# Dense layer of a fused attention, expert and dense kernel: activation buffers of 8 blocks, another order of the products, and a square that reads PSUM

## The chip, the cores and the metric

The kernel runs on one core of a Trainium2 chip. The metric is the device time of one execution in microseconds (us). Engines: PE is TensorE (matmuls), ACT is ScalarE, DVE is VectorE, POOL is GpSimd, SP issues most of the DMAs. [...]

## What is computed

Attention with queries pooled by two, then a layer of 8 experts with one expert for each token, then a dense layer. The change touches the dense layer alone:

```python
def _moe2_ref(x, w_in, w_out):      # x 2304 x 512, w_in 512 x 2048, w_out 2048 x 512
    h = x @ w_in
    r = np.maximum(h, 0.0)
    g = r * r
    return (g @ w_out).astype(np.float32)

def reference(**kwargs):
    ...
    attn_out = _attn_ref(**attn_kwargs)
    x = np.ascontiguousarray(attn_out.transpose(0, 2, 1, 3)).reshape(B * S, H * D)
    x = _moe_ref(x=x, **moe_kwargs)
    return _moe2_ref(x=x, **moe2_kwargs)
```

## The kernel before

Each f32 operand is held as two 16-bit halves, high and low, and each product is three matmuls (high x high, high x low, low x high). The dense layer is class Ffn. Its tokens are cut into 6 token blocks of 384 (N), the 2048 hidden columns into 16 blocks f of 128.

A first product of token block tt and column block f, here called a group, is the method hidden: 12 matmuls of 384 columns into one PSUM bank (L1465), then a relu on ACT into r in SBUF (L1470), the square on DVE in place (L1471), and one group later the high half on ACT (L1482) and the low half on POOL (L1483), which go to gh and gl. r has 3 buffers. The banks come from two pools, ps_b with 3 and ps_a with 2, chosen by f modulo 5. The function first(tt) runs the groups of a token block; of block 0 the first 8 (F1) have been done already, between the steps of the expert stage, into the tile fill (method step, the same hidden).

The function second(tt) makes three tiles of 128 tokens, each of 48 matmuls of 512 columns into a bank of ps_o (L1543); DVE scales the result (L1550) and POOL scatters it to the output with an indirect DMA (L1553).

The weights w_out arrive as 64-bit numbers in 16 blocks of 128 rows and are converted while first(0) and first(1) run: for each block three DVE instructions that put an f32 together (L1154, L1159, L1163), a copy of the high half on ACT (L1168) and a subtraction for the low half on POOL (L1170). The generator convert has six steps for each block (one is empty), and every group of the token blocks 0 and 1 takes four of them. The DMA of a later block (L1147) is issued by SP when a block is converted.

The instructions of each engine run in the order in which the program issues them; there is no planner in this part, the loops at the end of the method run are the order. All of them first do first(0), then first(tt + 1) ahead of second(tt). gh and gl of a token block are one tile each, of all 16 blocks, with two buffers.

Of the kernel before, what the change touches and what calls it, by code (L numbers as in the profile page):

```python
# [8 lines left out]
F32 = mybir.dt.float32  # L9
F16 = mybir.dt.float16  # L10
# [4 lines left out]
ALU = mybir.AluOpType  # L15
# [579 lines left out]
NTOK = 2304  # L595
# [3 lines left out]
F1 = 8  # L599
# [40 lines left out]
def half(w, lo):  # L640

    return w.bitcast(BF16) if lo else w
# [162 lines left out]
class Moe:  # L805
# [592 lines left out]
    def hidden(self, f2, ps, w1, x, w):  # L1398

        for f in range(2):  # L1400
            m = 0
            for k in range(4):
                fs = slice(256 * k + 128 * f, 256 * k + 128 * f + 128)
                for wh, xh in ((0, 0), (0, 1), (1, 0)):
                    self.nc.tensor.matmul(  # L1405
                        out=ps[:, f, 0:w], lhsT=w1(wh, f2)[:, fs], rhs=x[:, 4 * xh + k, 0:w],
                        start=(f == 0 and m == 0), stop=(m == 11), skip_group_check=True,
                    )
                    m += 1
# [15 lines left out]
class Ffn:  # L1425
# [3 lines left out]
    N = 384  # L1429
# [28 lines left out]
    def hidden(self, tt, f, ps, r, gh, gl):  # L1458
        nc = self.nc
        c0 = slice(tt * self.N, tt * self.N + self.N)  # L1460
        fs = slice(128 * f, 128 * f + 128)
        m = 0
        for k in range(4):
            for wh, yh in ((0, 0), (0, 1), (1, 0)):
                nc.tensor.matmul(  # L1465
                    out=ps, lhsT=half(self.win[wh][:, k, fs], wh), rhs=self.yT[yh][:, k, c0],
                    start=(m == 0), stop=(m == 11),
                )
                m += 1
        nc.scalar.activation(out=r, in_=ps, func=ACTF.Relu)  # L1470
        nc.vector.tensor_tensor(out=r, in0=r, in1=r, op=ALU.mult)  # L1471
        self.pend.append((r, gh, gl))
        if len(self.pend) > 1:
            self.halves()
# [10 lines left out]
    def run(self, ctx):  # L1485
        nc, moe, N = self.nc, self.moe, self.N
        pool = lambda n, b, **kw: ctx.enter_context(moe.tc.tile_pool(name=n, bufs=b, **kw))
        stg = pool("stg2", 2)
        one = pool("one", 1)
        gp = pool("gp", 2)  # L1490
        rp = pool("rp", 3)
        ps_o = pool("ps_o", 3, space=PSUM, reuse_waits="tile")
        ps_b = pool("ps_b", 3, space=PSUM, reuse_waits="tile")
        ps_a = pool("ps_a", 2, space=PSUM, reuse_waits="tile")
        wout = [one.tile([128, 16, 512], F16, name=f"wo{i}") for i in range(2)]
        cm = one.tile([128, 18, 2], F32, name="cms")
        nc.sync.dma_start(out=cm, in_=moe.cm.rearrange("(t p) m -> p t m", p=128))  # L1497
        ti = one.tile([128, 18], I32, name="ti")
        nc.vector.tensor_copy(out=ti, in_=cm[:, :, 1])
        so = {}  # L1500

        def wout_load(n):
            so[n] = stg.tile([128, 1024], U32, tag="g64", name="g64")
            moe.load64(so[n], moe.w_out[128 * n:128 * n + 128, :], nc.sync)

        def convert():
            for n in range(16):
                f = stg.tile([128, 512], U32, tag="f32", name="f32")
                split = moe.split64(so.pop(n), f, wout[0][:, n], wout[1][:, n])
                for i, _ in enumerate(split):  # L1510
                    yield
                    if i == 2:
                        yield
                if n + 2 < 16:
                    wout_load(n + 2)
                yield

        wout_load(0)
        wout_load(1)
        conv = convert()  # L1520
        G = {}

        def first(tt):
            gh, gl = G[tt] = [gp.tile([128, 16, N], F16, tag=t, name=t) for t in ("gh", "gl")]
            for f in range(0 if tt else F1, 16):
                ps = (ps_a if f % 5 in (3, 4) else ps_b).tile([128, N], F32, tag="a", name="a")
                r = rp.tile([128, N], F32, tag="r", name="r")
                self.hidden(tt, f, ps, r, gh[:, f], gl[:, f])
                if tt < 2:
                    for _ in range(4):  # L1530
                        next(conv, None)
            self.finish()

        def second(tt):
            g = G.pop(tt)
            at = lambda l, f: g[l][:, f] if tt or f >= F1 else self.g0[:, l, f]
            for rt in range(3):
                ps = ps_o.tile([128, 512], F32, tag="o", name="o")
                rs = slice(128 * rt, 128 * rt + 128)
                m = 0  # L1540
                for f in range(16):
                    for l, wh in ((0, 0), (0, 1), (1, 0)):
                        nc.tensor.matmul(  # L1543
                            out=ps, lhsT=at(l, f)[:, rs], rhs=half(wout[wh][:, f], wh),
                            start=(m == 0), stop=(m == 47),
                        )
                        m += 1
                n = 3 * tt + rt
                o = rp.tile([128, 512], F32, tag="o", name="ot")
                nc.vector.tensor_scalar(  # L1550
                    out=o, in0=ps, scalar1=cm[:, n, 0:1], scalar2=None, op0=ALU.mult
                )
                nc.gpsimd.indirect_dma_start(  # L1553
                    out=moe.out, out_offset=bass.IndirectOffsetOnAxis(ap=ti[:, n:n + 1], axis=0),
                    in_=o, in_offset=None, bounds_check=NTOK - 1,
                )

        first(0)
        for tt in range(NTOK // N):
            if tt + 1 < NTOK // N:  # L1560
                first(tt + 1)
            second(tt)


class First:
# [317 lines left out]
```

## Time and profile before

| | |
|---|---|
| median of 3 runs | 1180.41 us (1174.77 to 1183.54) |
| profiled execution, its own time | 1168.99 us |
| its span, first to last instruction | 1167.0 us |
| mean granted PE clock | 0.948 of full speed |
| busy share of the span: PE, DVE, ACT, POOL | 90%, 63%, 45%, 45% |

The span is what the trace covers; the execution's time has 2.0 us around it. Shares of busy time are means over stages with different limits, attention first, then the experts, then from about 771 us the dense layer. The views below give times in us from the start of the span. An instruction is named by engine and line, out<-in by the program's tiles; what stands in brackets behind it is the idle time of its engine before it and what ended that. [...]

### The profile page before, as it was taken

What the parts mean: (1) busy time and instruction counts of PE and PEld (TensorE: products, weight loads), DVE (VectorE), ACT (ScalarE), POOL (GpSimd) and SP (SyncE); (2) the same over time, 40 slices, a digit from 0 to 9 for tenths busy, and PEclk for the clock granted to TensorE, in tenths of its full rate; (3) what the DMA queues carried; (4) which work ended last, traced back from release to release, by engine and by line L of the source; (5) the groups of instructions that cost most, each with busy time, mean ns of one, the idle gap of its engine ahead of it and who ended that gap; (6) DMA issues with size and microseconds to landing.
All of it is one profiled execution on the core that took longest, in us unless ns stands there. A gap on an engine that the chain in (4) does not pass through costs nothing. (4 is left out here: it accounts for less than half of the span.)

```text
span 1167.0 us, 28582 instructions
## 1 busy us (share of the span) xinstructions
PE 1046.6 (90%) x11297; PEld 702.0 (60%) x11340; DVE 734.8 (63%) x1403; ACT 521.7 (45%) x972; POOL 519.3 (45%) x454
## 2 busy tenths in 40 slices
PE   6889999988999798999998869787879999999996
PEld 2455665655666466999898858654435454555543
DVE  6898999999999988866654547958822121211200
ACT  4777777767777566323222325533303131221300
POOL 3655564555666456522442336826623232232300
PEclk7899998999999898999999889989889999999999
DMA  7555875755675435659558595323300000000000
GB/s 195 141 130 145 201 169 108 170 147 118 140 151 150 72 96 161 166 176 224 103 111 210 135 256 167 89 72 111 111 19 10 19 10 10 19 10 19 1 28 27
DMA packets 166245, 128.17 MB, mean 110 GB/s; under 512 B 125208, under 2 KB 129432, under 8 KB 166064
## 3 DMA queue, kind: packets, MB, share of 16 engines
q1 hardware_dynamic: 160304, 107.91, 39.0%
q0 software_dynamic: 5760, 17.85, 5.0%
q8 instruction: 113, 1.85, 0.7%
q14 instruction: 68, 0.56, 0.2%
HBM read 74.69 MB, written 12.60 MB: 75 GB/s over the span
## 5 line engine op out<-in xcount | busy, mean ns | idle before, releaser
L422 POOL TENSOR_TENSOR pl<-p 128x512 f16<-128x512 f32 x144 | 167.9, 1170 | 176.2 <-ACT p L412 173.3
L394 PE MATMUL st<-r,t 128*128 128x64 f16 (+3 forms) x1152 | 202.6, 299 | 5.4 <-ACT p L412 4.7
L412 ACT ACTIVATE p<-st 128x512 f32<-128x512 f32 x288 | 168.5, 595 | 78.9 <-PE st L394 77.1
L1465 PE MATMUL a<-yT,win 128*128 128x384 f16 x1056 | 178.5, 332 | 16.8 <-ACT r L1470 11.8
L459 PEld LDWEIGHTS <-p 128*128 128x128 bf16 x2304 | 135.6, 99 | 68.1 <-issue 18.5
L1465 PEld LDWEIGHTS <-win 128*128 128x128 f16 (+1 forms) x1152 | 114.8, 100 | 97.3 <-issue 27.1
L459 PE MATMUL pv<-vx,p 128*128 128x65 f16 x2250 | 160.0, 197 | 9.5 <-DVE xb L500 9.5
L1543 PE MATMUL o<-wo,gh 128*128 128x512 f16 (+1 forms) x513 | 154.5, 380 | 5.7 <-ACT wo L1168 4.2
L459 PE MATMUL pv<-vx,pl 128*128 128x65 f16 x1125 | 144.9, 194 | 0.0
L422 DVE TENSOR_TENSOR pl<-p 128x512 f16<-128x512 f32 x144 | 141.8, 985 | 1.0 <-ACT p L412 0.7
L1470 ACT ACTIVATE r<-a 128x384 f32<-128x384 f32 x88 | 42.9, 487 | 194.8 <-PE a L1465 128.7
L1483 POOL TENSOR_TENSOR gl<-r,gh 128x384 f16<-128x384 f32 x88 | 87.3, 997 | 79.8 <-ACT gh L1482 79.8
L1471 DVE TENSOR_TENSOR r<-r 128x384 f32<-128x384 f32 x88 | 59.5, 676 | 100.2 <-ACT r L1470 100.2
L364 DVE CUSTOM_DVE_ANT_0 rd<-sm,rd,mc 128x512 bf16<-128x512 f32 x144 | 106.7, 744 | 22.4 <-PE sm L338 9.1
L1405 PE MATMUL fsm<-x,ws 128*128 128x192 f16 (+1 forms) x1344 | 104.7, 241 | 17.6 <-issue 9.8
L1550 DVE TENSOR_SCALAR ot<-o,cms 128x512 f32<-128x512 f32 x18 | 13.5, 751 | 166.5 <-PE o L1543 166.5
L394 PEld LDWEIGHTS <-t 128*128 128x128 f16 (+1 forms) x1152 | 77.0, 100 | 66.5 <-issue 32.0
L1405 PEld LDWEIGHTS <-ws 128*128 128x128 f16 (+1 forms) x1344 | 100.6, 101 | 20.8 <-issue 12.2
L459 PEld LDWEIGHTS <-pl 128*128 128x128 f16 x1152 | 111.0, 101 | 0.0
L361 ACT ACTIVATE rd<-sm 128x512 bf16<-128x512 f32 x144 | 85.5, 597 | 52.7 <-PE sm L338 43.6
L1417 PEld LDWEIGHTS <-ws 128*128 128x128 f16 (+1 forms) x1344 | 97.5, 99 | 18.1 <-issue 14.5
L1417 PE MATMUL fst<-hl,ws 128*128 128x192 f16 (+1 forms) x448 | 96.9, 236 | 12.7 <-issue 8.8
(249 smaller groups left out, 1735.3 us busy)
## 6 DMA issues: line engine op xcount, KB each, us to landing
stg<-in_moe_w SPq DMA_DIRECT2D x24, 1024.0 KB, 7.7
vr<-in_v SPq DMA_DIRECT2D x16, 576.0 KB, 4.2
kr<-in_k SPq DMA_DIRECT2D x15, 576.0 KB, 5.3
fill<-in_moe_w_in POOLq DMA_DIRECT2D x16, 512.0 KB, 7.0
g<-in_moe_w_out SPq DMA_DIRECT2D x16, 512.0 KB, 3.5
qr<-in_q SPq DMA_DIRECT2D x15, 512.0 KB, 5.7
t<-t SPq DMA_DIRECT2D x16, 288.0 KB, 3.8
xs<-tmp SPq DMA_DIRECT2D x16, 192.0 KB, 2.8
```

What stands on the lines that cost most here:

```text
L361: nc.scalar.activation(out=s["rd"], in_=ps, func=ACTF.Relu)
L364: nc.vector.tensor_tensor_reduce(out=rd, in0=ps, in1=rd, scale=1.0, scalar=mc[:, slots:slots + 1], op0=ALU.add, op1=ALU.max, accum_out=mx[ ...
L394: nc.tensor.matmul(out=st[:, j * n:j * n + n], lhsT=lhs[0:kk, m, :], rhs=r[0:kk, c0:c0 + n], start=first, stop=(kk == 65), skip_group_chec ...
L412: nc.scalar.activation(out=p, in_=st[:, 0:p.shape[1]], func=ACTF.Exp, scale=SCALE)
L422: eng.tensor_tensor(out=pl, in0=s.pop(("p32", i)), in1=s["ph", i], op=ALU.subtract)
L459: nc.tensor.matmul(out=o[:, 0:vn], lhsT=s[p, i][:, cs:cs + w], rhs=vx[:, 9 * a_ + c, v0:v0 + vn], start=(u == 0 and p == "ph" and v0 == 0) ...
L1405: self.nc.tensor.matmul(out=ps[:, f, 0:w], lhsT=w1(wh, f2)[:, fs], rhs=x[:, 4 * xh + k, 0:w], start=(f == 0 and m == 0), stop=(m == 11), s ...
L1417: self.nc.tensor.matmul(out=yp[m // 2][:, m % 2, 0:w], lhsT=w2(wh, f)[:, ds], rhs=h(l, f), start=(f == i == m % 2 == 0), stop=(f == 7 and ...
L1465: nc.tensor.matmul(out=ps, lhsT=half(self.win[wh][:, k, fs], wh), rhs=self.yT[yh][:, k, c0], start=(m == 0), stop=(m == 11),)
L1471: nc.vector.tensor_tensor(out=r, in0=r, in1=r, op=ALU.mult)
L1483: self.nc.gpsimd.tensor_tensor(out=lo, in0=g, in1=hi, op=ALU.subtract)
L1543: nc.tensor.matmul(out=ps, lhsT=at(l, f)[:, rs], rhs=half(wout[wh][:, f], wh), start=(m == 0), stop=(m == 47),)
```

## The change

Three things change in the dense layer. The square becomes one DVE instruction that takes max(a, 0) from the PSUM bank and multiplies it with r from SBUF, where before it multiplied r with itself. gh and gl become tiles of 8 column blocks with five buffers, in place of 16 blocks with two; the scaled output tile has two buffers in place of three. And the order becomes first of 0, 1, 2, second of 0, second of 1, first of 3, second of 2, first of 4, second of 3, first of 5, second of 4, second of 5. With it the conversion of w_out goes along with the groups of token blocks 0, 1 and 2, three steps with each.

```diff
--- before.py
+++ after.py
@@ -1468,7 +1468,9 @@
                 )
                 m += 1
         nc.scalar.activation(out=r, in_=ps, func=ACTF.Relu)
-        nc.vector.tensor_tensor(out=r, in0=r, in1=r, op=ALU.mult)
+        nc.vector.scalar_tensor_tensor(
+            out=r, in0=ps, scalar=0.0, in1=r, op0=ALU.max, op1=ALU.mult
+        )
         self.pend.append((r, gh, gl))
         if len(self.pend) > 1:
             self.halves()
@@ -1487,7 +1489,7 @@
         pool = lambda n, b, **kw: ctx.enter_context(moe.tc.tile_pool(name=n, bufs=b, **kw))
         stg = pool("stg2", 2)
         one = pool("one", 1)
-        gp = pool("gp", 2)
+        gp = pool("gp", 5)
         rp = pool("rp", 3)
         ps_o = pool("ps_o", 3, space=PSUM, reuse_waits="tile")
         ps_b = pool("ps_b", 3, space=PSUM, reuse_waits="tile")
@@ -1520,20 +1522,25 @@
         conv = convert()
         G = {}
 
+
+
         def first(tt):
-            gh, gl = G[tt] = [gp.tile([128, 16, N], F16, tag=t, name=t) for t in ("gh", "gl")]
+            g = G[tt] = {}
             for f in range(0 if tt else F1, 16):
+                if f % 8 == 0:
+                    g[f // 8] = [gp.tile([128, 8, N], F16, tag=t, name=t) for t in ("gh", "gl")]
+                gh, gl = [a[:, f % 8] for a in g[f // 8]]
                 ps = (ps_a if f % 5 in (3, 4) else ps_b).tile([128, N], F32, tag="a", name="a")
                 r = rp.tile([128, N], F32, tag="r", name="r")
-                self.hidden(tt, f, ps, r, gh[:, f], gl[:, f])
-                if tt < 2:
-                    for _ in range(4):
+                self.hidden(tt, f, ps, r, gh, gl)
+                if tt < 3:
+                    for _ in range(3):
                         next(conv, None)
             self.finish()
 
         def second(tt):
             g = G.pop(tt)
-            at = lambda l, f: g[l][:, f] if tt or f >= F1 else self.g0[:, l, f]
+            at = lambda l, f: g[f // 8][l][:, f % 8] if tt or f >= F1 else self.g0[:, l, f]
             for rt in range(3):
                 ps = ps_o.tile([128, 512], F32, tag="o", name="o")
                 rs = slice(128 * rt, 128 * rt + 128)
@@ -1546,7 +1553,7 @@
                         )
                         m += 1
                 n = 3 * tt + rt
-                o = rp.tile([128, 512], F32, tag="o", name="ot")
+                o = rp.tile([128, 512], F32, tag="o", name="ot", bufs=2)
                 nc.vector.tensor_scalar(
                     out=o, in0=ps, scalar1=cm[:, n, 0:1], scalar2=None, op0=ALU.mult
                 )
@@ -1556,10 +1563,13 @@
                 )
 
         first(0)
-        for tt in range(NTOK // N):
-            if tt + 1 < NTOK // N:
-                first(tt + 1)
+        first(1)
+        first(2)
+        second(0)
+        for tt in range(1, NTOK // N):
             second(tt)
+            if tt + 2 < NTOK // N:
+                first(tt + 2)
 
 
 class First:
```

## Rows read from the trace of the kernel before

**Rows 1.** The chain that ended last: start us, us, engine, line, times.

```profile
878.08 31.20 PE a L1465 x192
909.55 10.95 PE o L1543 x50
...
940.36 31.20 PE a L1465 x192
```

**Rows 2.** Windows: us; PE, PEld, DVE, ACT, POOL busy; clock; DMA.

```profile
800.00:810.00 10.00, 8.75 (x53) 5.06 (x52) 8.82 (x11) 3.81 (x9) 5.87 (x5) 1.00 0.36 105
```

**Rows 3.** Waits in 771 to 860: us in total, times, longest us.

```profile
PE a L1465 <- ACT r L1470: 11.8, 7, 2.1
...
PE o L1543 <- ACT wo L1168: 4.2, 2, 2.4
...
PE o L1543 <- POOL wo L1170: 1.5, 2, 0.9
```

**Rows 4.** Timeline of PE and ACT at the start: start us, us, instruction.

```profile
774.36 17.87 PE L1465 MATMUL a<-yT,win 128*128 128x384 f16 x101 [1.98 <-issue]
...
777.44 0.49 ACT L1470 ACTIVATE r<-a 128x384 f32<-128x384 f32 x1 [8.15 <-DMA g<-in_moe_w_out]
```

**Rows 5.** Timeline of DVE, one cycle: start us, us, instruction.

```profile
795.92 1.23 DVE L1471 TENSOR_TENSOR r<-r 128x384 f32<-128x384 f32 x1 [1.07 <-ACT r L1470]
797.08 1.13 DVE L1154 TENSOR_SCALAR f<-g 128x512 uint32<-128x512 uint32 x1
798.24 1.28 DVE L1159 SCALAR_TENSOR_TENSOR f<-g,f 128x512 uint32<-128x512 uint32 x1
799.56 0.69 DVE L1163 SCALAR_TENSOR_TENSOR f<-g,f 128x512 uint32<-128x512 uint32 x1
800.17 0.55 DVE L1471 TENSOR_TENSOR r<-r 128x384 f32<-128x384 f32 x1
800.64 0.42 DVE L1154 TENSOR_SCALAR f<-g 128x512 uint32<-128x512 uint32 x1
801.10 1.60 DVE L1159 SCALAR_TENSOR_TENSOR f<-g,f 128x512 uint32<-128x512 uint32 x1
802.62 1.26 DVE L1471 TENSOR_TENSOR r<-r 128x384 f32<-128x384 f32 x1
803.81 0.68 DVE L1163 SCALAR_TENSOR_TENSOR f<-g,f 128x512 uint32<-128x512 uint32 x1
805.56 1.24 DVE L1471 TENSOR_TENSOR r<-r 128x384 f32<-128x384 f32 x1 [1.07 <-ACT r L1470]
```

**Rows 6.** Timeline of DVE at the start of the conversion.

```profile
778.89 0.69 DVE L1159 SCALAR_TENSOR_TENSOR f<-g,f 128x512 uint32<-128x512 uint32 x1
```

**Rows 7.** Timeline of ACT, POOL and DVE around 791 us.

```profile
790.64 0.63 ACT L1168 ACTIVATE wo<-f 128x512 f16<-128x512 f32 x1 [2.58 <-DVE f L1163]
791.18 0.47 ACT L1470 ACTIVATE r<-a 128x384 f32<-128x384 f32 x1
...
791.35 1.16 POOL L1170 TENSOR_TENSOR wo<-f,wo 128x512 bf16<-128x512 f32 x1 [2.02 <-ACT wo L1168]
...
791.45 1.60 DVE L1159 SCALAR_TENSOR_TENSOR f<-g,f 128x512 uint32<-128x512 uint32 x1
```

**Rows 8.** Single lines, all instances: duration ns min/median/max, first and last start.

```profile
L1295 DVE SCALAR_TENSOR_TENSOR hl<-fsm,hh x56: 493/551/559, 516.7 to 765.2; 128x384 f16<-128x384 f32 x56
...
L1471 DVE TENSOR_TENSOR r<-r x88: 551/559/1266, 778.0 to 1096.7; 128x384 f32<-128x384 f32 x88
L1471 DVE TENSOR_TENSOR fillr<-fillr x8: 544/559/2423, 686.9 to 765.7; 128x384 f32<-128x384 f32 x8
...
L1483 POOL TENSOR_TENSOR gl<-r,gh x88: 908/915/1362, 780.3 to 1098.1; 128x384 f16<-128x384 f32 x88
```

**Rows 9.** Windows of 2.5 us, PE alone: us, busy, clock, DMA.

```profile
813.00:815.50 2.50, 0.38 (x3) 1.00 0.24 28
...
825.50:828.00 2.50, 2.50 (x9) 0.50 0.39 149
```

## Prediction

> **What bounds the kernel now.** I read the windows of the dense layer first, then the table of waits, then the timelines of each engine. The layer occupies the last 396 us. From 878 us to the end TensorE (PE) runs without a gap: 16 groups of 12 first products take 31.20 us, which is 1.95 us for each group, and the second products of one token block take 940.36 - 909.55 = 30.81 us [rows 1]. That stretch can't be shortened by a change of order. The loss lies before it, from 771 to 878 us, where the blocks of w_out are converted. There VectorE (DVE) is busy 8.82 of 10 us and PE waits [rows 2]; PE's waits name ScalarE (ACT) and GpSimd (POOL), 11.8 us on the relu that hands back a PSUM bank, then 4.2 and 1.5 us on the converted weights themselves, which second products of block 0 reach before they exist [rows 3]. Both are one cause: all of it queues behind DVE.
>
> How large is the loss? PE starts in earnest at 774.36 and the first relu can start at 777.44 [rows 4], so group 0 ends at about 777.4. From there PE needs 39 more groups for the first products of blocks 0, 1 and 2 (block 0 has only 8 left), 39 x 1.95 = 76.1, and 2 x 30.8 = 61.6 for the second products of blocks 0 and 1: it could be through at 915.0. It is through at 940.36, the end of second of block 1 [rows 1]. So 25.3 us are lost, and no more can be won here.
>
> Why is DVE full? One cycle of before is three groups and two w_out blocks, 9.64 us from 795.92 to 805.56 [rows 5]. Its nine instructions show two lengths for the same work: the square 0.55 or 1.23 and 1.26, L1154 0.42 or 1.13, L1159 0.69 [rows 6] or 1.28 and 1.60. The longer ones lie beside POOL's subtractions: L1159 began at 791.45, the POOL instruction at 791.35 took 1.16 [rows 7], and the DVE instruction ended 1.60 later. In the cycle five DVE instructions are held, by 0.68, 0.71, 0.59, 0.91 and 0.71, 3.6 us together, and POOL has five instructions in it (three gl, two wo): about 0.72 a hit.
>
> **The change part by part.** *The square.* It takes max(a,0) from PSUM and r from SBUF in place of r twice. The kernel before has the same kind of instruction, L1295: PSUM in0, SBUF in1, 128x384, in a stage where POOL works too. Its 56 instances run from 493 to 559 ns, median 551; the square from SBUF has median 559 and a maximum of 1266 [rows 8]. So I cost the instruction itself at nothing and the hits on it as gone. [...]
>
> *What the square now holds.* PSUM is released by DVE's square and no longer by ACT's relu. Where DVE is idle this is 0.6 us later, with three to five banks of 1.95 us each in turn: hidden. In the conversion stretch the square stands behind L1154, L1159 and L1163, and PE stands behind the square; that is in the sum below.
>
> *Three steps of conversion for each group in place of four.* A w_out block has six steps (L1154, L1159, L1163, an empty one, ACT's L1168, POOL's L1170). So one block now goes with two groups (a pair) in place of one and a half; 16 pairs are 32 of the 40 groups. Within a pair there is a closed loop, since ACT and DVE work in order: L1163 ends; ACT's L1168 starts 0.04 later and the next relu 0.54 after that (790.64 to 791.18), 0.47 long [rows 7]; then square 0.55, L1154 0.42, L1159 0.69, L1163 0.69: 3.4 us, where hand-overs and overlaps about cancel. PE needs 3.90 for a pair, so unhindered PE would be the bound. But POOL has three instructions for each pair. Its wo starts 0.71 after L1168 and ends 1.87 after it; relu and square are done 1.56 after it, so L1154 waits 0.3. By then two gl are due (0.91 each undisturbed [rows 8]), and they alternate with DVE: one hit on L1159 and one on L1163, each 0.59, the row in which a gl hit L1159. No row shows L1163 hit, nor L1154 hit by the tail of a wo. The turn is 3.4 + 0.3 + 0.6 + 0.6 = 4.9 us. Bounds: 3.90 if nothing is hit, and 3.4 + 0.91 + 0.72 + 0.72 = 5.75 if all three are hit at their longest. I take 4.9; nearest to it is the rate of before, 9.64/2 = 4.82 for a w_out block.
>
> So the conversion doesn't get shorter; PE gets two groups done in each turn in place of one and a half, and no second product stands in front of unfinished weights.
>
> *The order.* L1163 of block 0 ends at about 778.89 + 0.69 + 0.69 = 780.3 [rows 6]. Fifteen turns of 4.9 later, at 853.8, that of block 15 ends; square 31 (counting groups from 0) follows, 854.4. Group 36 takes the PSUM bank of group 31, so groups 36 to 39 run from there: 7.8 us, to 862.2. Then second of blocks 0 and 1, whose weights all exist by then (ACT and POOL need another 2 us after 853.8): 61.6 us, to 923.8. Against 940.36 that is **16.5 us less**. After that point both orders are the same list (first of 3, second of 2, and so on), so the end moves by as much. With 3.90 a turn, PE bound, the point is 915.0 (25.3 less), with 5.75 it is 780.3 + 86.3 + 0.6 + 7.8 + 61.6 = 936.5 (3.9 less).
>
> *Queues that are passed.* The output scatters of block 0 (POOL) move behind the subtractions of block 2; nobody reads them. The w_out loads on SP's queue are issued two blocks ahead, 9.8 us at the new rate, 9.64 before: hidden as before. The scaled output tile has two buffers in place of three, used every 10.3 us against some 4 us for scale and scatter: hidden.
>
> *Buffers of 8 blocks.* Block 0 fills one of five, blocks 1 and 2 two each, so first of 2 finds room; first of 3 takes those of block 0 and half of block 1, read by then by products that stand ahead of it on PE itself. No wait.
>
> *The eight squares in the expert stage.* One of them was held to 2.42 us; the median is 0.56 [rows 8]. [...] I take 0.4.
>
> *The clock.* PE idles about 1 us in each turn, and it did about that in 800 to 810 [rows 2] at full clock. It fell to half (825.5 to 828) after a stretch like 813 to 815.5, where PE was busy for 0.38 of 2.5 us [rows 9]. Waits that long are not left in the sum, so I take nothing; two such falls would cost 2.5 us at most, mostly covered by banks in hand.
>
> Sum: 16.9 us. The profiled execution took 1168.99 (span 1167.0, 2.0 around it), 11.4 less than the median of the three runs; it would become 1152. The stages that differ among runs are not touched, so I take the same 16.9 from the median 1180.41: **1163.5 us**.
>
> **The rivals.** *PE becomes the bound:* POOL's gl fall beside ACT-paced gaps and hit nothing. 25.3 + 0.4 less, 1154.7. For it: the wait-free loop is 3.4 against 3.9. Against it: in before DVE is hit by every POOL instruction of the cycle. Chance 0.12.
>
> *The square doesn't get free of POOL* (the change doesn't do what it is written for): three hits at their longest for each turn, 5.75, 3.9 less, 1176.5. For it: no row shows this instruction with f32 in both inputs. Against it: 56 of L1295 without one long one. Chance 0.11.
>
> *Slower:* the short waits, repeated in all 32 groups, hold PE at half clock. A group then takes 3.90 and PE is the bound: 40 groups 156 us, the end of second of 1 at 775.4 + 156 + 61.6 = 993, 53 us later than before, about 1230. It decides from roughly 13 groups at half clock (25.3/1.95): there the result is as before. Against it: from 778 us to the end half clock lasted 2.5 us at a time in slices like that of [rows 9] and 5 at most, and came after longer waits. Chance 0.03.
>
> **How the numbers follow.** The forecast has 0.74. Its own spread is some 4 us from the turn (0.25 us x 15) and some 4 from the runs (before: 1174.77 to 1183.54), so 1157 to 1170. The range reaches to PE bound below and part way to the held square above: 1155 to 1173. About 1% (12 us) is what a measurement here can tell from no change; the line is at 1168.6. Faster by over 1%: most of the forecast (0.60) and PE bound (0.12), 0.72. Within 1%: the rest of the forecast and the held square, 0.25. Slower: 0.03.
>
> **What would show it.** In the profile after: L1471 near 0.55 us with no instance near 1.2; DVE's repeat at 4.9 us for each L1163; PE's waits from 780 to 855 shared out in pieces under 1 us, and no wait of L1543 on L1168 or L1170; second of block 0 starting near 862 and the last matmul some 16 us earlier. A repeat near 4 would be PE bound, near 5.8 the held square. The prediction is wrong if a turn is lengthened by something off this list, such as the bank rotation at the seam of two token blocks, or if half clock stays.

## The result, and the profile after

The kernel with the change takes 1161.97 us (median of four runs, 1158.82 to 1168.05), the one before 1177.84 in the runs taken with it: 15.9 us less, ratio 0.9867, 95% interval 0.9825 to 0.9909. In a second comparison it is 1158.96 against 1173.16, ratio 0.9886 (0.9841 to 0.9932). The ratios and intervals are taken from the fast runs alone, so they need not be the quotient of the medians, which are over all runs. The forecast was 16.9 us less, 1163.5 from a median of 1180.41.

Behind the square the line numbers of the changed kernel are higher: gl's subtraction, L1483 before, is L1485, and the second products, L1543 before, are L1550.

The spans of the two profiled executions differ by 8.2 us only, 1167.0 and 1158.8. That is no contradiction: attention and the experts took longer in the second one. The first relu of the dense layer's own loop starts at 777.44 before [rows 4]; ACT's timeline of the changed kernel has it here:

```profile
783.27 0.49 ACT L1470 ACTIVATE r<-a 128x384 f32<-128x384 f32 x1 [8.72 <-DMA g<-in_moe_w_out]
```

In all the executions profiled for this study it lies between 773.2 and 792.1, though the program up to it differs in eight groups of the dense layer at most. So traces are compared below from that relu on, and times by the medians. In the kernel before, second of token block 1 ends 940.36 - 777.44 = 162.9 us after the first relu [rows 1]. In the changed kernel first of 3 is what follows it; the chain that ended last (start, us, line, times) has it at

```profile
932.25 31.20 PE a L1465 x192
```

932.25 - 783.27 = 149.0 us after the first relu. The layer is 13.9 us shorter; the forecast said 16.5. What the timed medians have beyond that lies inside their spread.

**One turn of DVE after** (its timeline; start us, us, instruction), which answers to the cycle of before [rows 5]:

```profile
826.14 0.56 DVE L1471 SCALAR_TENSOR_TENSOR r<-a,r 128x384 f32<-128x384 f32 x1 [0.61 <-ACT r L1470]
826.62 0.63 DVE L1154 TENSOR_SCALAR f<-g 128x512 uint32<-128x512 uint32 x1
827.28 1.28 DVE L1159 SCALAR_TENSOR_TENSOR f<-g,f 128x512 uint32<-128x512 uint32 x1
828.60 1.29 DVE L1163 SCALAR_TENSOR_TENSOR f<-g,f 128x512 uint32<-128x512 uint32 x1
829.81 0.55 DVE L1471 SCALAR_TENSOR_TENSOR r<-a,r 128x384 f32<-128x384 f32 x1
830.96 0.56 DVE L1471 SCALAR_TENSOR_TENSOR r<-a,r 128x384 f32<-128x384 f32 x1 [0.61 <-ACT r L1470]
```

From square to square of the same kind it is 830.96 - 826.14 = 4.82 us, two groups and one block of w_out (L1154, L1159, L1163). Both squares are short. L1159 and L1163 have 1.28 and 1.29 in place of the 0.69 they take alone: each was held once, by about 0.6. L1154 is held by 0.21. The single lines tell that all squares are short, against a maximum of 1266 and 2423 ns before [rows 8]; min, median and max ns:

```profile
L1471 DVE SCALAR_TENSOR_TENSOR r<-a,r x88: 543/558/559, 783.8 to 1088.6; 128x384 f32<-128x384 f32 x88
L1471 DVE SCALAR_TENSOR_TENSOR fillr<-fpv,fillr x8: 542/557/558, 691.6 to 771.6; 128x384 f32<-128x384 f32 x8
```

**PE after** (timeline of PE). It runs 44.75 us without a wait, then waits 0.76 twice, and then once for 5.57 us, on the square:

```profile
780.07 44.75 PE L1465 MATMUL a<-yT,win 128*128 128x384 f16 x261 [2.53 <-issue]
825.59 4.06 PE L1465 MATMUL a<-yT,win 128*128 128x384 f16 x24 [0.76 <-DVE r L1471]
830.41 4.06 PE L1465 MATMUL a<-yT,win 128*128 128x384 f16 x24 [0.76 <-DVE r L1471]
840.04 30.04 PE L1465 MATMUL a<-yT,win 128*128 128x384 f16 x168 [5.57 <-DVE r L1471]
869.92 5.34 PE L1550 MATMUL o<-wo,fill 128*128 128x512 f16 x24
```

With the three matmuls ahead of the first row, 3 + 261 + 24 + 24 = 312 matmuls are done up to there, 26 groups. The next one is the third of token block 2 (f = 2). The pools of PSUM are chosen by f modulo 5, and where a block ends, f = 15, 0, 1 and 2 all fall to ps_b with its three banks: f = 2 needs the bank of f = 15, only three groups back, where inside a block a group needs the one five back. This place, where two token blocks meet, is called the seam below. The fourteen groups behind it take 30.04 us, not 14 x 1.95 = 27.3. Windows of 2.5 us say why (us; PE busy; granted clock; DMA share, GB/s):

```profile
835.00:837.50 2.50, 0.00 (x0) 1.00 0.64 197
837.50:840.00 2.50, 0.00 (x0) 0.70 0.03 13
840.00:842.50 2.50, 2.46 (x8) 0.50 0.60 206
842.50:845.00 2.50, 2.50 (x9) 0.50 0.01 3
845.00:847.50 2.50, 2.50 (x17) 0.94 0.62 200
```

In two whole windows there is no matmul. In the second of them the granted clock falls (0.70 on average), and when PE starts again it runs at half clock for 5 us and a little more (0.50 from 840.00 to 845.00, 0.94 in the window behind). The kernel before has such falls too (0.50 from 825.50 to 828.00 [rows 9]).

### The profile page after: what moved, and what is told of

It is laid out like the page before. It is cut to its first block, busy times and chain, and to the rows that moved or that the text cites. A ratio compares the mean times of both kernels' runs of the same rounds, so it can differ in the third digit from the quotient of the medians.

```text
span 1158.8 us, 28570 instructions
## 1 busy us (share of the span) xinstructions
PE 1047.6 (90%) x11297; PEld 703.5 (61%) x11340; DVE 725.9 (63%) x1403; ACT 520.6 (45%) x972; POOL 524.5 (45%) x454
## 5 line engine op out<-in xcount | busy, mean ns | idle before, releaser
L422 POOL TENSOR_TENSOR pl<-p 128x512 f16<-128x512 f32 x144 | 170.3, 1187 | 178.0 <-ACT p L412 175.9
L1550 PE MATMUL o<-wo,gh 128*128 128x512 f16 (+1 forms) x513 | 153.8, 379 | 0.0
L422 DVE TENSOR_TENSOR pl<-p 128x512 f16<-128x512 f32 x144 | 137.5, 956 | 1.8 <-ACT p L412 1.4
L1485 POOL TENSOR_TENSOR gl<-r,gh 128x384 f16<-128x384 f32 x88 | 87.5, 1003 | 68.7 <-ACT gh L1484 68.5
L1405 PE MATMUL fsm<-x,ws 128*128 128x192 f16 (+1 forms) x1344 | 101.7, 236 | 14.6 <-issue 10.6
L1417 PE MATMUL fst<-hl,ws 128*128 128x192 f16 (+1 forms) x448 | 99.4, 241 | 13.3 <-issue 7.2
L1417 PE MATMUL fst<-hh,ws 128*128 128x192 f16 (+1 forms) x896 | 103.6, 241 | 3.4 <-DVE ws L1256 3.1
```

Source lines behind the costliest of these rows:

```text
L422: eng.tensor_tensor(out=pl, in0=s.pop(("p32", i)), in1=s["ph", i], op=ALU.subtract)
L1405: self.nc.tensor.matmul(out=ps[:, f, 0:w], lhsT=w1(wh, f2)[:, fs], rhs=x[:, 4 * xh + k, 0:w], start=(f == 0 and m == 0), stop=(m == 11), s ...
L1417: self.nc.tensor.matmul(out=yp[m // 2][:, m % 2, 0:w], lhsT=w2(wh, f)[:, ds], rhs=h(l, f), start=(f == i == m % 2 == 0), stop=(f == 7 and ...
L1485: self.nc.gpsimd.tensor_tensor(out=lo, in0=g, in1=hi, op=ALU.subtract)
L1550: nc.tensor.matmul(out=ps, lhsT=at(l, f)[:, rs], rhs=half(wout[wh][:, f], wh), start=(m == 0), stop=(m == 47),)
```

## Experiments

Times inside the layer count from its first relu; the turn is the distance from the end of the first L1163 to that of the last, divided by 15; the column before the ratio is the start of the last matmul.

| kernel | turn us | to second of block 0 | to the last matmul | ratio to before (95%) |
|---|---|---|---|---|
| before | 4.83 | 60.4 | 380.5 | |
| changed | 4.86 | 86.7 | 366.5 | 0.9867 (0.9825 to 0.9909) |
| changed, again | 4.87 | 86.8 | 366.6 | 0.9886 (0.9841 to 0.9932) |
| square alone | 4.31 | 54.2 | 372.4 | 0.9909 (0.9871 to 0.9947) |
| order alone | 5.45 | 91.5 | 371.4 | 0.9925 (0.9885 to 0.9966) |
| four steps | 4.27 | 95.0 | 374.9 | 0.9934 (0.9894 to 0.9974) |
| gl filled with zeros | 4.42 | 79.6 | 359.5 | one run |
| no gl | 3.90 | 75.8 | 355.7 | one run |
| banks by a running count | 4.86 | 84.1 | 364.0 | 0.9882 (0.9834 to 0.9930) |
| 12 steps in 5 groups | 5.25 | 77.2 | 357.1 | 0.9810 (0.9765 to 0.9856) |
| both of these | 5.21 | 75.9 | 355.7 | 0.9818 (0.9769 to 0.9867) |

The theory was that POOL's subtractions hold DVE instructions with two SBUF inputs, that this sets the turn, and that the change wins by taking the square out of it and by giving PE two groups in a turn. Rivals: the source of the square is neutral; the order wins by itself, as second of block 0 no longer meets unfinished weights; the turn is set by something else in the loop through ACT and the banks.

**The square alone.** The kernel before with

```diff
-        nc.vector.tensor_tensor(out=r, in0=r, in1=r, op=ALU.mult)
+        nc.vector.scalar_tensor_tensor(
+            out=r, in0=ps, scalar=0.0, in1=r, op0=ALU.max, op1=ALU.mult
+        )
```

> The kernel before with the new square alone (max of PSUM times r); order, buffers and the four steps for each group as before. Theory of the shared hit (POOL's subtractions lengthen DVE instructions with two SBUF inputs, and the square gets out of it): all 88 squares at 0.55 us, DVE's cycle of three groups falls from 9.64 to some 9.0 us, the layer is 7 to 8 us shorter. Rival (the square's source is neutral, only the order of products matters): cycle 9.6, within 2 us of before.

DVE's timeline, one cycle of three groups from square to square:

```profile
811.77 0.56 DVE L1471 SCALAR_TENSOR_TENSOR r<-a,r 128x384 f32<-128x384 f32 x1 [1.07 <-ACT r L1470]
812.25 0.64 DVE L1154 TENSOR_SCALAR f<-g 128x512 uint32<-128x512 uint32 x1
812.92 1.28 DVE L1159 SCALAR_TENSOR_TENSOR f<-g,f 128x512 uint32<-128x512 uint32 x1
814.24 1.28 DVE L1163 SCALAR_TENSOR_TENSOR f<-g,f 128x512 uint32<-128x512 uint32 x1
815.45 0.54 DVE L1471 SCALAR_TENSOR_TENSOR r<-a,r 128x384 f32<-128x384 f32 x1
...
820.37 0.56 DVE L1471 SCALAR_TENSOR_TENSOR r<-a,r 128x384 f32<-128x384 f32 x1 [1.08 <-ACT r L1470]
```

820.37 - 811.77 = 8.60 us in place of 9.64, below the 9.0 expected; the layer is 8.1 us shorter. The hits of POOL don't all vanish, some move on: L1163, at 0.69 in every instance before, is now held to 1.28 in one block of a cycle and to 0.93 in the other. What the square gained was thereby partly given back, and still the cycle lost a microsecond. The source is not neutral. Nor is it the form of the instruction that frees the square: L1159 and L1163 have the same form (SCALAR_TENSOR_TENSOR), with both inputs in SBUF, and are held, to 1.28 each in the rows above.

**The order alone**, the changed kernel with the old square (the diff above, reversed).

> The changed kernel with the old square (r times r in SBUF); order, buffers of 8 blocks and three steps as in the change. Theory of the shared hit: squares up to 1.27 us again, a turn of two groups takes 5.3 to 5.5 us in place of 4.83, and the layer is 6 to 8 us shorter than before, so that the two halves of the change add up. Rival (order is all): as the changed kernel, 14 us shorter in the layer. Second rival (PSUM held by DVE costs): faster than the changed kernel.

```profile
815.82 1.24 DVE L1471 TENSOR_TENSOR r<-r 128x384 f32<-128x384 f32 x1 [0.61 <-ACT r L1470]
816.98 1.13 DVE L1154 TENSOR_SCALAR f<-g 128x512 uint32<-128x512 uint32 x1
818.15 1.29 DVE L1159 SCALAR_TENSOR_TENSOR f<-g,f 128x512 uint32<-128x512 uint32 x1
819.47 0.69 DVE L1163 SCALAR_TENSOR_TENSOR f<-g,f 128x512 uint32<-128x512 uint32 x1
820.08 0.55 DVE L1471 TENSOR_TENSOR r<-r 128x384 f32<-128x384 f32 x1
821.24 1.24 DVE L1471 TENSOR_TENSOR r<-r 128x384 f32<-128x384 f32 x1 [0.61 <-ACT r L1470]
```

821.24 - 815.82 = 5.42 us for a turn: one square of two is held to 1.24 and L1154 to 1.13. The layer is 9.1 us shorter than before, a little more than expected, and the turn is 0.58 longer than with the new square. Alone the halves give 8.1 and 9.1 us, 17.2 in sum; together they gave 13.9, and 16.5 with the long wait at the seam taken out (below). So they nearly add up once that wait is gone. The order does win something by itself, but not all, and whether it does so by sparing the second products a wait for weights is tested further down.

**What lengthens the turn.** First POOL's subtraction for gl was replaced by a fill, which reads nothing:

```diff
-        self.nc.gpsimd.tensor_tensor(out=lo, in0=g, in1=hi, op=ALU.subtract)
+        self.nc.gpsimd.memset(lo, 0.0)
```

> The changed kernel, with POOL's subtraction for the low half of the activations replaced by a fill with zeros, which reads no SBUF; the low half is left out of the result. Theory of the shared hit: L1159 and L1163 lose their long form of 1.28 us but for what wo hits, a turn falls from 4.83 to 3.9 to 4.2 us (PE's own pace), second of block 0 starts 8 to 11 us earlier against the start of the layer. Rival (the turn is set by the closed loop through ACT, DVE and the PSUM banks, whatever POOL reads): turn 4.6 or more.

```profile
800.49 1.34 DVE L1154 TENSOR_SCALAR f<-g 128x512 uint32<-128x512 uint32 x1
801.86 0.69 DVE L1159 SCALAR_TENSOR_TENSOR f<-g,f 128x512 uint32<-128x512 uint32 x1
802.59 0.69 DVE L1163 SCALAR_TENSOR_TENSOR f<-g,f 128x512 uint32<-128x512 uint32 x1
...
799.68 1.16 POOL L1170 TENSOR_TENSOR wo<-f,wo 128x512 bf16<-128x512 f32 x1 [2.48 <-ACT wo L1168]
800.78 0.77 POOL L1485 MEMSET gl<- 128x384 f16 x2
```

L1159 and L1163 are at 0.69, as expected, but the turn is 4.42, more than the 4.2 allowed: L1154 has grown to 1.34. It lasts through the rest of wo and both fills, which end at 801.55, and ends 0.28 later. So the expectation missed that a fill can hold L1154, and the run did not yet tell POOL from the rest of the loop. The next one takes the instruction away, and gl's tile with it (a line that the diff below doesn't have); second products read the high half twice, so that all their matmuls remain:

```diff
-        self.nc.gpsimd.tensor_tensor(out=lo, in0=g, in1=hi, op=ALU.subtract)
...
-            at = lambda l, f: g[f // 8][l][:, f % 8] if tt or f >= F1 else self.g0[:, l, f]
+            at = lambda l, f: g[f // 8][0][:, f % 8] if tt or f >= F1 else self.g0[:, 0, f]
```

> The changed kernel without POOL's instruction for the low half of the activations (second products take the high half in its place; the low half is left out of the result). In the run with fills in its place L1154 was held by the fills. Theory (POOL's instructions are all that lengthens the turn beyond PE's 3.90 us): L1154 at 0.7 or less, L1159 and L1163 at 0.69, turn 3.9 to 4.0 us, PE without a wait, first relu to second of block 0 in 76 to 77 us. Rival (something else in the loop through ACT holds it at 4.4): 4.4 as with the fills.

```profile
800.90 0.42 DVE L1154 TENSOR_SCALAR f<-g 128x512 uint32<-128x512 uint32 x1
801.35 0.69 DVE L1159 SCALAR_TENSOR_TENSOR f<-g,f 128x512 uint32<-128x512 uint32 x1
802.07 0.69 DVE L1163 SCALAR_TENSOR_TENSOR f<-g,f 128x512 uint32<-128x512 uint32 x1
802.68 0.55 DVE L1471 SCALAR_TENSOR_TENSOR r<-a,r 128x384 f32<-128x384 f32 x1
804.32 0.56 DVE L1471 SCALAR_TENSOR_TENSOR r<-a,r 128x384 f32<-128x384 f32 x1 [1.09 <-ACT r L1470]
804.80 0.42 DVE L1154 TENSOR_SCALAR f<-g 128x512 uint32<-128x512 uint32 x1
```

Every DVE instruction has its short form, the turn is 3.90 us, PE's own pace for two groups, and PE has no wait up to second of block 0. The loop through ACT and the banks costs nothing beyond PE's pace. This is the theory's strongest support: all of the 0.96 us by which a turn exceeds PE's pace goes away with POOL's gl. It could also have acted by keeping the buffers of r, which it reads, from the next relu. The waits of the changed kernel speak against that: from 790 to 860 us no wait of ACT or DVE names POOL, the relu's two waits, 1.5 us in sum, are for PE.

**The order without the slower pace.**

```diff
-                    for _ in range(3):
+                    for _ in range(4):
```

> The changed kernel with four steps of conversion for each group, as before the change, in place of three; order, square and buffers as changed. Theory (the order gains only by giving PE more groups in each turn): the turn of one and a half groups stays at 4.3 us, as with the square alone, the conversion ends 8 us earlier than in the changed kernel, and yet second of block 0 starts 6 to 9 us later, 93 to 96 us after the first relu; the layer is 5 to 8 us shorter than before, as with the square alone. Rival (the order gains by keeping second of block 0 away from unfinished weights, 5.7 us of waits): within 2 us of the changed kernel.

All as the theory had it: turn 4.27, second of block 0 after 95.0 us, layer 5.6 us shorter. The new order with the old pace is 2.5 us behind the square alone with the old order, though no product waits for weights in it. PE's timeline shows the loss in front of them, a wait at nearly each group and 6.46 us at the seam:

```profile
838.79 2.11 PE L1465 MATMUL a<-yT,win 128*128 128x384 f16 x12 [0.38 <-DVE r L1471]
842.44 2.11 PE L1465 MATMUL a<-yT,win 128*128 128x384 f16 x12 [1.54 <-DVE r L1471]
844.89 2.11 PE L1465 MATMUL a<-yT,win 128*128 128x384 f16 x12 [0.33 <-DVE r L1471]
853.46 29.05 PE L1465 MATMUL a<-yT,win 128*128 128x384 f16 x168 [6.46 <-DVE r L1471]
```

The 14 groups of the last row take 29.05 us, 1.7 more than 27.3. No view shows the granted clock here; that it was half clock again, and that much of the 2.5 us, is the author's estimate from the changed kernel, where the 14 groups took 30.04 us behind a wait of 5.57, with the clock at 0.50. Without these 1.7 this order would still not be ahead. So the 5.7 us which before was spent waiting for weights [rows 3] is no gain of its own; the order helps by making room for 32 groups beside the conversion.

**The seam.** The changed kernel again beside three others, and the banks chosen by a count that doesn't start over:

> The changed kernel once more, beside the next three on one chip: about 1.3% faster than before, and again one wait of PE of 5 to 6 us on the square at the third group of token block 2, with half clock behind it.

```diff
-                ps = (ps_a if f % 5 in (3, 4) else ps_b).tile([128, N], F32, tag="a", name="a")
+                ps = (ps_a if (16 * tt + f) % 5 in (3, 4) else ps_b).tile([128, N], F32, tag="a", name="a")
```

> The changed kernel with the PSUM pool of a group chosen by a running count of groups in place of f, so that no four groups in a row share the pool of three banks where two token blocks meet. Theory (that seam makes the one long wait, and the half clock behind it costs 2.7 us): no wait over 1.5 us, no half clock between 785 us and second of block 0, 2 to 3 us less than the changed kernel. Rival (DVE's turn sets the end, the wait is only gathered in one place): the start of second of block 0 within 1 us of the changed kernel's.

The changed kernel did repeat itself, with its wait of 5.6 us. With the running count:

```profile
773.05 44.72 PE L1465 MATMUL a<-yT,win 128*128 128x384 f16 x261 [1.71 <-issue]
818.54 4.06 PE L1465 MATMUL a<-yT,win 128*128 128x384 f16 x24 [0.77 <-DVE r L1471]
823.36 4.06 PE L1465 MATMUL a<-yT,win 128*128 128x384 f16 x24 [0.76 <-DVE r L1471]
...
852.59 7.96 PE L1465 MATMUL a<-yT,win 128*128 128x384 f16 x48 [0.76 <-DVE r L1471]
```

One window over the whole stretch (us; PE busy; granted clock; DMA share, GB/s):

```profile
785.00:860.00 75.00, 68.47 (x414) 1.00 0.30 91
```

The one wait has become eight, 6.4 us in sum and 1.04 at most (the two rows in the middle stand for that pattern), the granted clock stays at 1.00 through all of them, and second of block 0 starts 2.5 us earlier (84.1 against 86.7 and 86.8). PE waits nearly as long in total (6.4 us against 7.1); what is saved is, in the main, the half clock. The medians of the two kernels, 1156.48 and 1158.96, can't tell 2.5 us apart; the trace does.

**A version that beats both.** If a turn takes 4.8 us whatever PE does, about 2.5 groups of PE (4.88 us) fit in it. The six steps of a block are dealt out over 2.5 groups, and the 96 steps fill all 40:

```diff
-                    for _ in range(3):
+                    for _ in range((2, 3, 2, 3, 2)[(16 * tt + f) % 5]):
```

> The changed kernel with 12 steps of conversion for each five groups (2, 3, 2, 3, 2) in place of three for each, so that the 96 steps fill all 40 groups. Theory (a turn lasts 4.8 us whatever PE does, so give it 2.5 groups, 4.88 us of PE): PE nearly without a wait, second of block 0 some 7 to 9 us earlier against the start of the layer, 2% faster than before. Rivals: POOL has half a subtraction more in each turn, the turn grows to 5.3 us or more and nothing is won; or second of block 0 waits for the last blocks of w_out.

```profile
776.44 51.83 PE L1465 MATMUL a<-yT,win 128*128 128x384 f16 x309 [1.62 <-issue]
829.50 27.46 PE L1465 MATMUL a<-yT,win 128*128 128x384 f16 x168 [1.23 <-DVE r L1471]
856.79 3.40 PE L1550 MATMUL o<-wo,fill 128*128 128x512 f16 x15
```

One wait of 1.23 us is left. The turn did grow, to 5.25, nearly as the first rival had it, while a turn now holds half a gl more; but the layer won 9.5 us all the same. PE's 2.5 groups need 4.88, so it gains 0.37 us on DVE in each turn, some 5.5 in 15 turns, and the banks in hand cover that. The wait that is left comes after 312 matmuls, at the seam with its three banks. DVE's last instruction of the conversion ends 83.5 us after the first relu, six after second of block 0 has started, and no product waits for it. With the running count too:

> Both of the last two edits. Theory: as the 12 steps alone, 0 to 2 us less, since PE has little left to wait for. Rival: the seam still costs half clock in that one, and this is 2 to 3 us faster.

```profile
780.28 79.25 PE L1465 MATMUL a<-yT,win 128*128 128x384 f16 x477 [2.40 <-issue]
859.37 5.34 PE L1550 MATMUL o<-wo,fill 128*128 128x512 f16 x24
```

477 + 3 matmuls are the 40 groups in one piece. Both versions are 1.8 to 1.9% faster than before, and can't be told apart by time; in the layer they are 9.5 and 10.8 us ahead of the changed kernel, 24.7 us ahead of before in the second case, of the 25.3 that the prediction took for all that could be won here.

## Why the prediction was right

- **Bound.** DVE in the conversion stretch, held by POOL: shown by the run without gl, where the turn falls from 4.86 to 3.90 us, PE's pace.
- **The square.** Forecast at nothing extra and out of POOL's way: 558 ns median and 559 at most in 88 instances, 559 median from SBUF before.
- **The turn.** Forecast 4.9 between 3.90 and 5.75; measured 4.86. By parts, in the turn shown above: 0.6 on L1159 and on L1163 as forecast, 0.21 on L1154 for 0.3. That L1163 would be hit was in no row of before; the run with the square alone and the changed kernel both show it.
- **The order.** Second of block 0 was forecast 862.2 - 777.4 = 84.8 us after the first relu; measured 86.7, and 84.1 with the running count of banks. This is the term that was mis-sized. The prediction took nothing for the clock, since "waits that long are not left in the sum", and named the bank rotation at the seam only as something off its list. It left a wait of 5.57 us there, against the sign "PE's waits from 780 to 855 shared out in pieces under 1 us", and the half clock behind it cost 30.04 - 27.3 = 2.7 us. The wait itself cost next to nothing, as DVE's turn set the end in either case. The other 0.7 us of the 2.6 that are missing lie in the second products of blocks 0 and 1, 62.3 us for 61.6. Most of that is a misreading of [rows 1]: the first products ahead of them end at 878.08 + 31.20 = 909.28, and the prediction counted from the row at 909.55, which starts later. A token block takes 940.36 - 909.28 = 31.1 us, two take 62.2. With that, what could be won at all is 24.7 us in place of 25.3, and the last version above wins it.
- **The eight squares in the expert stage.** No run shows the 0.4 us taken for them. All are at 0.54 to 0.56 us now, where before the median was 0.56 and the longest 2.42 [rows 8], and what that gave in time can't be read out of a stage whose end varies by many microseconds.
- **The rivals.** The held square is refuted by the single line. PE as the bound came true only in the versions with less POOL work or a slower conversion in each turn (3.90 us a turn without gl; one wait of 1.23 us, or none, with 12 steps in five groups). Half clock came once behind 785 us, with PE at work in it for 5 us (0.50 from 840.0 to 845.0); it never took hold. The prediction's readings of the clock before were loose, though. Half clock lasted nearly 7 us there at one point (the windows from 850.5 to 860.5 have 0.82, 0.50, 0.50 and 0.81), not 5 at most. And the fall of [rows 9] came behind the wait that ended at 824.88, not behind the one in the window from 813.
- **Luck.** The timed difference, 15.9 us for 16.9, agrees better than the layer does, 13.9 for 16.5; the rest is the spread of the runs ahead of the layer (the second comparison has 14.2).

## What to carry to other kernels

Where two engines hold each other up, count the hits in one repeat: taking one instruction out of the way can move the hit to the next one in line, and the gain is the difference (with the square alone L1163 went from 0.69 to 1.28 and 0.93, and the cycle still fell from 9.64 to 8.60). Background work that runs at a fixed pace should be dealt out over as many units of the bounding engine as there are, here 40 groups and not 24 or 32; an order that makes more room was worth nothing here until the pace used it (with four steps the last matmul starts at 374.9 us, with the old order at 372.4). And where buffers rotate by an index that starts over, look at the seam: one wait of 5.57 us had a clock of 0.50 behind it here, 6.4 us of waits in eight pieces left it at 1.00.

## What the runs showed of the hardware that was not expected

A POOL fill that reads nothing holds L1154, an instruction on uint32 with one SBUF input that takes 0.42 us for 512 elements alone (1.34 beside two fills of 0.4 us each and the end of wo). It is held beside subtractions too (1.13 with the order alone), so the theory's "two SBUF inputs" is too narrow. Eight waits of 0.76 to 1.04 us left the granted clock at 1.00, one of 5.57 us was followed by 0.50 for some 5 us. The length of a wait alone doesn't tell: before, of two waits of 2.12 us, the clock stayed at 1.00 behind the one that ended at 815.23 and was at 0.50 behind the one that ended at 824.88. And the stages ahead of the layer end anywhere between 773 and 792 us in executions of nearly the same program, which is why differences of 2 to 3 us had to be read inside the layer.
